# Third chunk's queries and keys ahead of the first gate product, row statistics of four chunks on ScalarE, small weight copies on VectorE

## The chip, the cores and the metric

The kernel runs on one core of one Trainium2 chip. The metric is the device time of one execution in microseconds. The kernel before takes 1048.6 us, the median of three runs (1048.55 to 1049.17). Engines are named as the profile names them: PE is TensorE's matmul (PEld its weight load), DVE is VectorE, ACT is ScalarE, POOL is GpSimd, SP is SyncE, which here issues the DMAs.

## The reference

2048 rows of 576 values go through two kinds of layer in turn, A, B, A, B, each on a layer norm of its input and with the input added back. A is attention with 32 heads of 18 values; a row looks at itself and at seven rows before it, two apart. B is two wide projections multiplied with each other and projected back.

```python
def _A_ref(x, wqkv, wo):                      # x: 1 x 2048 x 576, wqkv: 576 x 1728
    q, k, v = ...                             # 32 heads of 18
    idx = pos[:, None] - arange(8) * 2        # the rows that a row looks at
    logits = einsum("bhsd,bhswd->bhsw", q, kg) * 18 ** -0.5
    attn = softmax(where(idx >= 0, logits, -1e9))
    return einsum("bhsw,bhswd->bhsd", attn, vg).reshape(B, S, D) @ wo

def _B_ref(x, w_gate, w_up, w_down):          # F = 4608
    return ((x @ w_gate) * (x @ w_up)) @ w_down

x = x + _A_ref(_layernorm(x), A_wqkv, A_wo)
x = x + _B_ref(_layernorm(x), B_w_gate, B_w_up, B_w_down)
x = x + _A_ref(_layernorm(x), A_wqkv, A_wo)
x = x + _B_ref(_layernorm(x), B_w_gate, B_w_up, B_w_down)
```

## The kernel before

**Tiling.** The rows are cut into tiles of 128. An attention job j takes one tile (j = 0 and 1) or two (j = 2 and up); this text calls job j the chunk j + 1, so j = 2 is the third chunk. `seq` lists the jobs: rows 0, 1, 2 to 3, then 4 to 5, 6 to 7 of the first layer pair, then chunks of the second pair and the first in turn. The gated layer B follows: `first_pair` for the first two chunks, `small` for chunks 3 to 5, `big` for 512 rows at a time after that.

**A chunk of attention** (`attention`, L525 to L963) has these steps:

- `head` (L419): layer norm and transposition. Per tile DVE takes two `bn_stats` over 288 columns and a `bn_aggr` (L424, L426). ACT makes rstd of all the tiles of the chunk as exp(-0.5 ln(var + eps)) (L430, L431). The tile is normalised by DVE (L448) if `dve` is set, otherwise by ACT (L442, L443), and transposed by PE through a PSUM bank with a copy by ACT (L460, L463) if `on_pe` is set, otherwise by a DMA that SP issues (L453). `head` runs twice per chunk: in front of the attention (LN1) and in front of layer B (LN2).
- `project` (L580): q, k and v by products with the permuted weight `wqkv`, each with four full parts of the contraction and a tail of 64 rows. For j = 0 and 1 they are written out in place (L599). For later chunks they are units (`as_unit`, L543, products at L551) that are put among the gate products of layer B, at places that `IN_GU` names.
- logits: DVE multiplies q with shifted k (L744, four products with two shifts each); PE sums over the head's values with the selection matrix `Esel` (L760); softmax on DVE and ACT (L798, L785, L828 or L841, L837, L846 to L852); PE spreads the weights to the head's values with `Bsel` (L863); DVE multiplies with v and adds (L912, L928). For j = 0 PE adds them up (L916, L917), and the division by the softmax sum comes at the end (L931, L934) with 1/sum from L834 to L836, spread at L879 and copied at L883.
- output projection with `wo_p` (L479 for j = 0, L951 otherwise), the input added, and the second `head`; for j = 0 all this is `tail_fast` (L468 to L512).

**Layer B.** A unit (`g_unit`, L1038) makes a gate and an up product in two PSUM banks (L1046, tails L1056), ACT copies the gate (L1000), ACT and DVE or DVE alone multiply (L1002 to L1005). `batch` (L1014) puts the 64-row tails of neighbouring units together. In `first_pair` the first `SOLO` = 6 units are made for the first chunk alone with 128 columns each product, then six joint units for both chunks with 256 columns, then six for the second chunk alone; the down products follow (L1100, L1101).

**The start.** `wqkv` arrives as five blocks of rows, k = 0 to 4, and its columns are permuted by copies (`permute`, L338; the copies run at L351): per k one for queries (t3 = 0), one for keys (1), a small one of 128 columns for the last two values of every head's queries and keys (3), and later the values (2, 4). POOL also makes the identity, zeros, `Esel` and `Bsel` (`mk_sel`, L368) and the mask `cap` (`mk_cap`, L381).

**What sets the order.** Every operation is given to a planner (`Plan`) with engine, a cost in ns, keys that it reads and writes, a priority (smaller goes first) and sometimes an operation that it must follow (`after`). `Plan.run` walks through time and always issues the operation that can start first, by its costs; ties go to the smaller priority, then to the older operation. Each engine then runs its operations in that fixed order, waiting where data are late. Operations of PE in layer B form a chain (`bb`, L981, `chain["pe"]`), so their order is that of the program. `warm` (L965, matmuls at L967) fills planned waits of PE with products on the identity until the first product of the chain. PSUM banks come from pools: "unit" (two pairs), "boot" (three banks), "pa" (one bank at first) and "ring" (all of them later); `hand_over` moves banks into the ring. The costs and the order of priorities around the change:

```python
cost = {"DVE": 50 + 35 * nd, "ACT": 60 + 64 * nd, "POOL": 200 + 106 * nd}[eng]
op("POOL", 3200, mk_sel, w=["sel"], prio=1)
LN1P = {2: 1.5, 3: 3, 4: 2, 5: 2.5, 6: 2.5, 7: 3, 8: 1, 1: 0.4}
ATP = {1: 3, 2: 2.5, 3: 2.5, 4: 3, 5: 3, 6: 2}
```

Of the kernel before, what the change touches and what calls it, by code (L numbers as in the profile page):

```python
# [10 lines left out]
ALU = mybir.AluOpType  # L11
# [130 lines left out]
def kernel(  # L142
# [34 lines left out]
    KACT, VENG = (1, 4), ('POOL', 'POOL', 'ACT', 'ACT', 'ACT')  # L177
# [5 lines left out]
    BLK, JOB_AT, SOLO = 4, (0, 2), 6  # L183
# [147 lines left out]
    def setup_b():  # L331
# [6 lines left out]
        def permute(k, t3, eng, prio, d0=0, nd=16, **kw):  # L338
            if t3 < 3:
                src = (wrav[:, k, :] if t3 == 2 else wraw[:, k, t3 * D:(t3 + 1) * D]).rearrange("p (h d) -> p d h", h=H)[:, d0:d0 + nd, :]  # L340
                dst = wqkv[:, k, t3 * 512 + d0 * H:t3 * 512 + (d0 + nd) * H].rearrange("p (d h) -> p d h", h=H)
                cost = {"DVE": 50 + 35 * nd, "ACT": 60 + 64 * nd, "POOL": 200 + 106 * nd}[eng]
            else:
# [3 lines left out]
                cost = {"DVE": 80 + 75 * m, "ACT": 160 + 130 * m, "POOL": 250 + 180 * m}[eng]  # L347
# [38 lines left out]
        op("POOL", 3200, mk_sel, w=["sel"], prio=1)  # L386
# [11 lines left out]
        op("POOL", 0, swap, r=[f"wq{t}_{k}" for t in (0, 1, 3) for k in range(KT)],  # L398
# [20 lines left out]
    def head(src, keys, nst, dst, dkeys, prio, ab, on_pe, mg, first=None, then=None, dve=False):  # L419
# [9 lines left out]
        def rs():  # L429
            nc.scalar.activation(rstd[:, 0:nst], mv[:, 0:nst, 1], ACT.Ln, bias=eps_t[:])  # L430
            nc.scalar.activation(rstd[:, 0:nst], rstd[:, 0:nst], ACT.Exp, scale=-0.5)  # L431
        op("ACT", 490, rs, r=mk + ["eps"], w=[f"rstd{ab}"], prio=prio, after=then)
        if not dve:
            o = op("DVE", 210, lambda: nc.vector.scalar_tensor_tensor(nmr[:, 0:nst], mv[:, 0:nst, 0], -1.0, rstd[:, 0:nst],
# [4 lines left out]
        for i in range(nst):  # L439
# [4 lines left out]
            if dve:  # L444
                def apply_v(i=i):
                    x = src(i)
                    for c, d_, m in ((0, 0, D), (KF * P, D, TL)):
                        nc.vector.tensor_scalar(xn[i][:, d_:d_ + m], x[:, c:c + m], mv[:, i, 0:1], rstd[:, i:i + 1], op0=ALU.subtract, op1=ALU.mult)  # L448
                op("DVE", 420, apply_v, r=[keys[i], *mk, f"rstd{ab}"], w=[f"xn{ab}{i}"], prio=prio)
# [75 lines left out]
    def attention(j, la, t0, nst, units=None):  # L525
# [5 lines left out]
        on_pe, pe_sum = j < 4, j < 2  # L531
        prio, mg = (1, 0) if fast else (ATP.get(j, 3), 200 if j < 5 else 1500)
# [5 lines left out]
        head(lambda i: xin[:, i0 + i, :], xin_k, nst, xnT_A, xk, LN1P.get(j, prio), 0, j < 3, mg, None,marks["evq"] if j == 1 else None, j < 3)  # L538
# [41 lines left out]
        def project(tag, au, bu, tl, ea, eb, dkeys):  # L580


            if units is not None:
# [32 lines left out]
            if fast:  # L616
# [14 lines left out]
                def values():  # L631
# [9 lines left out]
                    for cost, fn, w_, eng in eb[2:]:  # L641
                        op("ACT", cost, lambda fn=fn: fn(ub, 0), r=[kb, "uv"], w=w_, prio=0.5, free="unit", use=ub)
# [95 lines left out]
        for p_ in range(W // 2):  # L738
# [27 lines left out]
            op("DVE", 60 + 5.6 * n, l1, r=qk, w=[pk], prio=lprio, after=marks["xb1"] if j == 1 and p_ == 3 else None)  # L766
# [35 lines left out]
        else:  # L802
# [20 lines left out]
            op("DVE", 100 + 7 * n, gather_l, r=[f"part{jj}" for jj in range(4)] + ["cap"], w=["Lt"], prio=prio - 1, margin=2500 if j < 5 else 3000)  # L823
            op("DVE", 240 + 4.5 * n, soft1d, w=["Lt", "mx", "rg"], prio=prio - 1)
        if fast:
            late["values"]()
            rz = xn_[1][1]
            op("ACT", 170 + 1.8 * n, lambda: nc.scalar.activation(late["a_c"][:, 0:W * sq], late["Lt"][:, 0:W * sq], ACT.Exp),  # L828
               r=["Lt"], w=["ac"], prio=0)

# [25 lines left out]
        if on_pe:  # L856
# [15 lines left out]
            if fast:  # L872
# [499 lines left out]
```

## Time and profile before

| | |
|---|---|
| median of three runs | 1048.6 us (1048.55 to 1049.17) |
| the profiled execution's own time | 1048.55 us |
| its span, first to last instruction | 1046.7 us |
| mean granted clock of PE | 0.998 |
| first gate product (L1046) starts | 33.54 us |
| PE busy from 34 to 100 us | 65.76 of 66 us |
| products on the identity (L967) | 107, 10.4 us |
| DMA | 135.5 MB, mean 129 GB/s |

A line of the profile's groups names the line of the code, the engine, the operation, what is written and what is read with shapes, the count, then the busy time and the mean of one, and the idle time of the engine in front of it with the one who ended it. In an order of time, a row has start and length in us; a square bracket behind it is the engine's idle time before it and its releaser. Matmul rows overlap, since they are pipelined: sixteen products of 128 columns start one behind the other in 0.89 us, though each row shows some 0.22 us.

### The profile page before, as it was taken

The page shows a single profiled execution, that of the slowest core. Times are in us where ns is not written, and L with a number is a line of the kernel's source. Part 1 is how long each engine was busy: PE and PEld are TensorE (multiplying, and loading weights), DVE is VectorE, ACT ScalarE, POOL GpSimd, SP SyncE. Part 2 cuts the span into 40 slices and gives each one's busy share as a digit, 9 for nine tenths or more (in the row PEclk, how much of TensorE's full clock was granted, in tenths as well). Part 3 has the DMA queues.
Part 4 walks back from the last instruction along what each step waited for, and adds up shares of the span by engine and source line. Part 5 has one row for each costly group of instructions (what it writes and reads, how often), then busy time and mean ns, then how long its engine had stood idle before and what let it go on. Part 6 is the DMA issues. An engine that isn't in the chain of part 4 may idle for free.

```text
span 1046.7 us, 19602 instructions
## 1 busy us (share of the span) xinstructions
PE 1028.5 (98%) x7898; PEld 595.9 (57%) x8016; DVE 723.0 (69%) x1366; ACT 446.3 (43%) x905; POOL 14.5 (1%) x54
## 2 busy tenths in 40 slices
PE   7999999999999999999999999999999999999998
PEld 6886886777765445554455544564455644554444
DVE  7896797889849886396766967579684796832211
ACT  4663763554645641354424443154531444214420
POOL 5000000000000000000000000000000000000000
PEclk9999999999999999999999999999999999999999
DMA  8918117454743805455143641635435352454212
GB/s 241 327 69 194 51 41 229 109 130 149 176 123 101 227 12 147 126 158 177 48 127 94 189 133 51 160 67 181 134 85 159 100 165 85 122 152 136 68 49 88
DMA packets 139834, 135.50 MB, mean 129 GB/s; under 512 B 43360, under 2 KB 137440, under 8 KB 139744
## 3 DMA queue, kind: packets, MB, share of 16 engines
q1 hardware_dynamic: 139744, 134.25, 45.0%
q8 instruction: 62, 1.02, 0.4%
q14 instruction: 28, 0.23, 0.1%
HBM read 114.49 MB, written 10.88 MB: 120 GB/s over the span
## 4 chain that ended last, share of the span: by engine, by line
PE 96%; issue 1%; DVE 1%; POOL 1%; ACT 0%; POOLq 0%; DVEq 0%
PE pu L1046 20%; PE pg L1046 18%; PE pg L1100 9%; PE pu L1100 8%; PE acct L1046 6%; PE pg L551 5%; PE pa L1046 4%; PE pu L551 4%; PE acct L1100 3%; PE pu L1056 3%; PE pg L1056 3%; PE pa L1100 2%; PE pg L1101 2%; PE pu L1101 2%; PE pa L951 1%
## 5 line engine op out<-in xcount | busy, mean ns | idle before, releaser
L1046 PEld LDWEIGHTS <-reg 128*128 128x128 bf16 x3072 | 277.5, 98 | 222.6 <-issue 24.2
L1046 PE MATMUL pu<-xnT_B,reg 128*128 128x512 bf16 (+2 forms) x1302 | 231.4, 316 | 1.3 <-issue 0.3
L1046 PE MATMUL pg<-xnT_B,reg 128*128 128x512 bf16 (+2 forms) x1204 | 220.4, 319 | 1.0 <-issue 0.2
L1100 PEld LDWEIGHTS <-reg 128*128 128x128 bf16 x864 | 84.4, 98 | 101.5
L1000 ACT CAST g_sb<-pu 128x512 bf16<-128x512 f32 x112 | 65.5, 588 | 126.3 <-PE pg L1056 66.2
L1003 DVE TENSOR_TENSOR reg<-reg,g_sb 128x512 bf16<-128x512 bf16 x144 | 59.7, 419 | 86.2 <-ACT reg L1002 76.6
L551 PEld LDWEIGHTS <-wqkv 128*128 128x128 bf16 (+1 forms) x1050 | 88.2, 97 | 34.0 <-issue 18.2
L744 DVE TENSOR_TENSOR prod<-qT,kT 128x2560 bf16<-128x2560 bf16 (+1 forms) x68 | 95.8, 1411 | 8.2 <-ACT kT L671 7.3
L912 DVE TENSOR_TENSOR prod<-vT,ab 128x1280 bf16<-128x1280 bf16 (+1 forms) x120 | 92.1, 776 | 0.0
L1000 ACT CAST g_sb<-pg 128x512 bf16<-128x512 f32 x112 | 65.8, 589 | 60.6 <-PE pu L1056 29.9
L928 DVE TENSOR_TENSOR qT<-qT,prod 128x1280 bf16<-128x1280 bf16 (+1 forms) x112 | 89.7, 801 | 2.5
L1101 PEld LDWEIGHTS <-reg 128*128 128x128 bf16 x864 | 84.9, 98 | 1.0
L430 ACT ACTIVATE rstd<-mv,eps_t 128x2 f32<-128x2 f32 (+1 forms) x33 | 9.8, 297 | 162.8 <-DVE mv L426 159.9
L1046 PE MATMUL acct<-xnT_B,reg 128*128 128x512 bf16 (+1 forms) x303 | 69.4, 354 | 0.5 <-issue 0.3
L551 PE MATMUL pg<-xnT_A,wqkv 128*128 128x256 bf16 (+1 forms) x500 | 69.6, 273 | 0.0
L1056 PE MATMUL pu<-xnT_B,reg 64*128 64x512 bf16 (+2 forms) x331 | 67.7, 316 | 0.1
L1101 PE MATMUL pu<-wd,reg 128*128 128x64 bf16 x336 | 64.8, 193 | 0.8
L1100 PE MATMUL pg<-wd,reg 128*128 128x512 bf16 x231 | 64.5, 380 | 0.0
L1056 PE MATMUL pg<-xnT_B,reg 64*128 64x512 bf16 (+2 forms) x305 | 62.8, 319 | 0.0
L551 PE MATMUL pu<-xnT_A,wqkv 128*128 128x256 bf16 (+1 forms) x410 | 59.1, 273 | 0.1
L1046 PE MATMUL pa<-xnT_B,reg 128*128 128x512 bf16 (+1 forms) x211 | 54.2, 376 | 0.6 <-issue 0.2
L1100 PE MATMUL pu<-wd,reg 128*128 128x512 bf16 x200 | 54.7, 380 | 0.0
(232 smaller groups left out, 1439.4 us busy)
## 6 DMA issues: line engine op xcount, KB each, us to landing
wd<-in_B_w_down_dram SPq DMA_DIRECT2D x152, 288.0 KB, 3.4
reg<-in_B_w_gate_dram SPq DMA_DIRECT2D x24, 768.0 KB, 4.8
reg<-in_B_w_up_dram SPq DMA_DIRECT2D x24, 768.0 KB, 6.3
reg<-in_B_w_down_dram SPq DMA_DIRECT2D x28, 288.0 KB, 3.3
s_dram<-s SPq DMA_DIRECT2D x13, 512.0 KB, 3.2
rg<-s_dram SPq DMA_DIRECT2D x52, 128.0 KB, 3.2
ab<-a_dram SPq DMA_DIRECT2D x52, 128.0 KB, 2.7
reg<-in_B_w_gate_dram SPq DMA_DIRECT2D x24, 96.0 KB, 5.6
```

The costliest lines, as they stand in the source:

```text
L430: nc.scalar.activation(rstd[:, 0:nst], mv[:, 0:nst, 1], ACT.Ln, bias=eps_t[:])
L551: nc.tensor.matmul(ring[use[p_]["slot"]][0:m, e * n:(e + 1) * n], lhsT=wqkv[r_, k, c0:c0 + m], rhs=xnT_A[r_, k, 0:n], start=start, stop=st ...
L744: nc.vector.tensor_tensor(late["prod"][lp(p_)][:, :, :, 0:n], q2, k2, op=ALU.mult)
L912: nc.vector.tensor_tensor(js(dst), js(vT[:, :, o0:o0 + n]), abw, op=ALU.mult)
L928: op("DVE", 60 + 3 * n, lambda tmp=tmp: nc.vector.tensor_tensor(oT[:, :, 0:n], oT[:, :, 0:n], tmp(), op=ALU.add), r=[pvk], w=ok, prio=prio)
L951: nc.tensor.matmul(b()[:, 0:HD], lhsT=oT[:, t, i * P:(i + 1) * P], rhs=wo_p[:, t, hh * HD:(hh + 1) * HD], start=(t == 0), stop=(t == KT - 1))
L1000: op("ACT", 590, lambda: nc.scalar.copy(g_sb[gs][:, 0:ul], bk(0)[:, 0:ul]), r=[keys[0]], w=[f"g{gs}"], prio=0, **fg)
L1003: op("DVE", 340, lambda: nc.vector.tensor_tensor(dst, dst, g_sb[gs][:, 0:ul], op=ALU.mult), r=[f"g{gs}"], w=[dk], prio=0)
L1046: nc.tensor.matmul(ring[use[q]["slot"]][:, e * n:(e + 1) * n], lhsT=w_[:, k], rhs=xT[:, k], start=(first and k == 0 and e == 0), stop=(las ...
L1056: nc.tensor.matmul(ring[use[q]["slot"]][:, e * n:(e + 1) * n], lhsT=w_[r_], rhs=xT[r_, KF], start=(fresh and e == 0), stop=not fresh, skip ...
L1100: nc.tensor.matmul(bank_of(i)[:], lhsT=lhs, rhs=wt[:, ft % 2, 0:512], start=first and not plus, stop=last_)
L1101: nc.tensor.matmul(tail_of(i), lhsT=lhs, rhs=wt[:, ft % 2, 512:D], start=(first and i == 0), stop=last_, skip_group_check=True)
```

## The change

The queries and keys of the third chunk (`PRE = 'q'`) are no longer units among the gate products: they are written out in the PE chain ahead of the first gate product. Their `head` may begin after the operation `weights` (1/sum of the first chunk). LN1 of chunks 2 to 5 (`LN1_S`) takes its row statistics on ACT, in two passes per tile with the accumulated output: the negated mean, then the sum of squares around it. The small copies of the weight go from POOL to DVE, the keys of k = 3 from DVE to ACT, and of the keys of k = 4 one half from ACT to POOL. LN2 of chunks 3 and 4 is transposed by DMA instead of PE (`LN2_PE` = 2 where 4 stood). `SOLO` is 7. The sixth and seventh chunk's units go to other places (`IN_GU`). The spread of 1/sum is written behind the fourth value product of the first chunk. Costs and priorities change.

```diff
-    KACT, VENG = (1, 4), ('POOL', 'POOL', 'ACT', 'ACT', 'ACT')
+    KENG = {1: ("ACT", "ACT"), 3: ("ACT", "ACT"), 4: ("ACT", "POOL")}
+    VENG = ('POOL', 'POOL', 'ACT', 'ACT', 'ACT')
+    LN1_PE, LN2_PE, ATT_PE, LN2_V, L1_LATE, MG, MGD = 3, 2, 4, 3, 3, 200, 3000
+    LN1_V = (0, 1, 2)
+    LN1_S, LN2_S = (1, 2, 3, 4), ()
+    PRE, SUM_PE = 'q', 2
+    LN1_AFTER = {1: "evq", 2: "weights"}
...
-    BLK, JOB_AT, SOLO = 4, (0, 2), 6
+    BLK, JOB_AT, SOLO = 4, (0, 2), 7
...
-                if t3 == 1 and k in KACT:
-                    for d0 in (0, 8):
-                        permute(k, t3, "ACT", 1.5, d0, 8)
+                if t3 == 1 and k in KENG:
+                    for d0, e_ in zip((0, 8), KENG[k]):
+                        permute(k, t3, e_, 1.5, d0, 8)
...
-                    permute(k, t3, "POOL" if t3 == 3 and k < KF else "DVE", 1.5)
+                    permute(k, t3, "DVE", 1.5)
...
-        op("POOL", 3200, mk_sel, w=["sel"], prio=1)
+        op("POOL", 3200, mk_sel, w=["sel"], prio=0.5)
...
+        def sums(i):
+            nc.scalar.activation(xn[i][:, 0:D], src(i), ACT.Copy, scale=-1.0 / D, accum_out=mv[:, i, 0:1])
+
+        def squares(i):
+            nc.scalar.activation(xn[i][:, 0:D], src(i), ACT.Square, bias=mv[:, i, 0:1], accum_out=mv[:, i, 1:2])
         for i in range(nst):
+            if act:
+                op("ACT", 820, lambda i=i: sums(i), r=[keys[i]], w=[f"sm{ab}{i}", f"mv{ab}{i}", f"xn{ab}{i}"], prio=prio, after=first)
+                op("ACT", 860, lambda i=i: squares(i), r=[keys[i], f"sm{ab}{i}"], w=[f"mv{ab}{i}", f"xn{ab}{i}"], prio=prio)
+                continue
...
-                op("DVE", 420, apply_v, r=[keys[i], *mk, f"rstd{ab}"], w=[f"xn{ab}{i}"], prio=prio)
+                op("DVE", 620, apply_v, r=[keys[i], *mk, f"rstd{ab}"], w=[f"xn{ab}{i}"], prio=prio)
...
-    LN1P = {2: 1.5, 3: 3, 4: 2, 5: 2.5, 6: 2.5, 7: 3, 8: 1, 1: 0.4}
-    ATP = {1: 3, 2: 2.5, 3: 2.5, 4: 3, 5: 3, 6: 2}
-    LPP = {1: 2.5, 2: 2, 3: 2.5, 4: 1.5, 5: 1.5, 6: 2}
+    LN1P = {1: 1.6, 2: 2, 3: 2.5, 4: 2.5, 5: 3, 6: 2.5, 7: 3, 8: 1.5}
+    ATP = {1: 2.5, 2: 2.5, 3: 3, 4: 2, 5: 2.5, 6: 1.5}
+    LPP = {1: 2.5, 2: 2.5, 3: 2.5, 4: 1.5, 5: 1.5, 6: 1.5}
...
-            if units is not None:
+            if units is not None and tag not in pre:
...
-        head(lambda i: xs_f[:, i0 + i, :], fk, nst, xT, xTk, (1 if j > 1 else 0.5) if j < JSM + 2 else prio - 1, 1, j < 4, mg, None, None, j < 3)
+        head(lambda i: xs_f[:, i0 + i, :], fk, nst, xT, xTk, (1 if j > 1 else 0.5) if j < JSM + 2 else prio - 1, 1, j < LN2_PE, mg, None, None, j < LN2_V, j in LN2_S)
...
+    if PRE:
+        early[2] = []
+        gens[2] = prepare(2, early[2], PRE)
+        next(gens[2])
...
-    IN_GU, IN_D = {0: {3: [2]}, 2: {0: [3], 7: [4]}, 3: {2: [5], 12: [6]}}, {}
+    IN_GU, IN_D = {0: {3: [2]}, 2: {0: [3], 7: [4]}, 3: {0: [5], 13: [6]}}, {}
```

More of the change, by code (lines that the diff above doesn't have):

```diff
@@ L397, in swap @@
             late["ab"] = rot.tile([P, 4, 2 * CH], BF16, name="ab")
-        op("POOL", 0, swap, r=[f"wq{t}_{k}" for t in (0, 1, 3) for k in range(KT)],
+        op("DVE", 0, swap, prio=0, r=[f"wq{t}_{k}" for t in (0, 1, 3) for k in range(KT)],
            w=["prod0", "prod1", "s10", "s11", "s12", "s13", "Lt", "ab", "ac", "rg"])
@@ L926, in attention, with spread_z, rzs @@
                     marks["sum"] = op("PE", 330, gather, r=[pvk, "ident"], w=[bo[0].key, bo[1].key], prio=0)
+                if i_ == 3:
+                    late["total"]()
+                    br = Bank()
+                    def spread_z():
+                        for e in range(4):
+                            for h_ in range(2):
+                                nc.tensor.matmul(br()[:, e * sq:(e + 1) * sq], lhsT=Bsel[:, e].rearrange("p a b -> p (a b)"),
+                                                 rhs=rz[:, h_ * sq:(h_ + 1) * sq], start=(e == 0 and h_ == 0), stop=(h_ == 1), skip_group_check=True)
+                    op("PE", 350, spread_z, r=["zs", "xn11", "sel"], prio=0, **br.take())
+                    def rzs():
+                        return late["Lt"][:, 2 * P:2 * P + n]
+                    op("ACT", 300, lambda: nc.scalar.copy(rzs(), br()[:, 0:n]), r=[br.key, "Lt"], w=["rzs"], prio=0.5, **br.drop())
             elif i_:
```

62 lines of the change are left out of this document (31 added, 31 removed).

## The prediction

> **What bounds the kernel now.** I read the page's busy shares first, then its chain of work that ended last, then the busy time by stage, then the order of time of the first 60 us.
>
> ```profile
> PE 1028.5 (98%) x7898; PEld 595.9 (57%) x8016; DVE 723.0 (69%) x1366; ACT 446.3 (43%) x905; POOL 14.5 (1%) x54
> PE 96%; issue 1%; DVE 1%; POOL 1%; ACT 0%; POOLq 0%; DVEq 0%
> ```
>
> TensorE (PE) carries 96% of the chain. The stages say where the rest is. Columns: window, length, then busy time of PE, PEld, DVE, ACT, POOL (in the last two rows PE alone), granted clock, DMA share, GB/s.
>
> ```profile
> 7.00:10.50 3.50, 0.61 (x8) 0.43 (x7) 3.15 (x7) 1.21 (x2) 3.44 (x15) 1.00 0.89 257
> 12.00:14.00 2.00, 2.00 (x23) 1.61 (x22) 0.12 (x1) 0.15 (x1) 2.00 (x9) 0.50 0.63 186
> ...
> 34.00:100.00 66.00, 65.76 (x877) 1.00 0.62 178
> 100.00:200.00 100.00, 99.58 (x939) 1.00 0.40 104
> ```
>
> From 34 us on PE misses 0.2 us in 66 and 0.4 in 100, and its list of waits there adds up to 1.2 us. So the time is the moment at which the first gate product starts, plus all PE work behind it. Only two things can help: an earlier or fuller start, and less PE work behind it. The start in order of time:
>
> ```profile
> 8.95 0.70 POOL L374 TENSOR_SCALAR_AFFINE_SELECT Bsel<-Bsel 128x128 bf16<-128x128 bf16 x1
> ...
> 10.51 1.10 POOL L351 COPY wqkv<-wraw 128x128 bf16<-128x128 bf16 x3
> 10.58 0.23 PE L599 MATMUL pu<-xnT_A,wqkv 128*128 128x128 bf16 x1 [2.97 <-POOL xf L307]
> ...
> 13.85 0.60 ACT L705 ACTIVATE qT<-pg 128x512 bf16<-128x512 f32 x1 [4.01 <-PE pu L599]
> ```
>
> The square bracket is the idle time before the row and who ended it. PE stands 2.97 us because GpSimd (POOL), which copies the small weight columns, first finishes the selection matrices: they run from 3.40 to 10.2 us, where the code's plan counts 3.2 us. The second stretch is ahead of the first gate product:
>
> ```profile
> 27.94 1.18 DVE L448 TENSOR_SCALAR xn<-xf,mv,rstd 128x576 bf16<-128x576 bf16 x4
> 29.03 0.82 DVE L744 TENSOR_TENSOR prod<-qT,kT 128x1280 bf16<-128x1280 bf16 x1
> 29.77 0.46 DVE L481 BATCH_NORM_STATS2 st<-pu 128x6 f32<-128x288 f32 x1
> 30.45 0.83 PE L967 MATMUL pa<-ident 128*128 128x128 bf16 x12 [0.78 <-ACT xnT_A L463]
> 33.54 1.09 PE L1046 MATMUL pg<-xnT_B,reg 128*128 128x128 bf16 x16
> ```
>
> L967 is padding on the identity. Between 27.9 and 33.5 PE does 1.3 us of output projection (first chunk), two transpose groups of 0.28, three groups of logit sums of about 0.25, one product of 0.28 on the identity, and else pads or waits: some 2.7 us are free.
>
> **The change part by part, on the profiled execution (1048.55 us; span 1046.7; the runs' median is 1048.6, so the same).**
>
> *Small copies to DVE, keys of k=3 to ACT, half of k=4 to POOL.* DVE loses one 128x512 copy (0.53 of a row of 8 in 4.26) and gains four small ones of 0.27 (the fifth is there already): +0.5, so its copies end at about 9.9 instead of 9.46, with the last weights in at 8.63. ACT does k=3 instead of one half of k=4: +0.6, in its idle stretch before 8.63. POOL loses four copies (0.40 each) and gains one of 128x256: between 0.40 (128x128) and 1.09 (128x512), on that line 0.63. It is queued behind the selection matrices (10.2), a memset of 0.09 and the cap memsets (0.55), so it ends near 11.4. PE can do k=0 to 3 before, and needs this piece for the nine closing products only: 11.65 to 12.3 instead of 13.20 to 13.85. **-1.5**. From one side -0.5 (POOL slower under the added DVE copies), from the other -3.5 (selections at their short rows' 0.7 and 0.25 us end at 8.4; then DVE's 9.9 decides). I take the middle one, because nothing in the change touches the selections. The granted clock is 0.50 from 11.5 to 15.0, behind the idle stretch, and that is why the nine products take 0.65 us. [...]
>
> *Row statistics on ACT for chunks 2 to 5.* Per 128-row tile DVE loses two rows of 0.44 and one of 0.21, 1.1 us; ACT gains two passes over 128x576. Nearest rows: the copy L463 of 128x640 at 0.69 and the normalisation L442 of 128x576 at 0.86; so 0.65 to 1.06 each, if reading the sum out is one more instruction at the 0.20 of the shortest row (L431). I take 0.86, the row of the same shape. [...] On the first chunk's path it frees DVE by a little: statistics stand directly ahead of the softmax maximum (18.73 to 19.54, maximum at 19.57). ACT's three value-weight copies now come before the second chunk's rstd (its priority goes from 0.4 to 1.6), so the transposed copy of the second chunk (0.69) lands at about 18.4, ahead of the exponential: +0.5 there, and -0.6 since the second chunk's normalisation (0.63 on DVE) no longer splits the four logit products. Together 0. Third chunk: four passes, 3.4 us, between 20.7 and 25.5 in ACT's idle 1.41, 1.44 and 0.92 us; its rstd is ready by about 26, as before (26.99).
>
> *The tail of the first chunk.* L448 now carries 620 instead of 420 in the plan (the rows say 0.43 + 0.29 less overlap, 0.6). With that the second chunk's product L744 at 29.03 falls behind the statistics it now holds up by 0.75 us. **-0.5**, between 0 and -0.8. First chunk ready for its gate product at 33.5 - 1.5 - 0.5 = 31.5.
>
> *Third chunk's q and k ahead of it.* In the profile they stand in L551: eight groups of four at 0.44, and four closing pairs at 0.11: 3.94 us of PE. They need both transposed tiles. Normalised at 26.4 to 27.6 (L448 less 1.5), tile one transposes behind the output projections (27.7), its copy takes 0.69, tile two uses the same PSUM bank (29.0), and its copy falls behind the first chunk's normalisation on ACT (30.4 to 31.1). So PE starts q and k at 31.1 and, with a group of logit sums between, the first gate product follows at 35.4, by order of the PE chain. The start moves from 33.5 to 35.4, **+1.9**; the work behind it loses **-3.94**, and one group of logit sums and one of transposes that now stand in 33.5 to 36.4 (0.24 + 0.28, **-0.5**).
>
> *Second normalisation of chunks 3 and 4 by DMA transposes.* 20 transposes on PE (L460) at 0.055 go: **-1.1**; four copies of 0.69 on ACT too. SP gains four transposes (1.2 to issue, 3.1 to land). Chunk 3 is normalised at 96.4 and used by PE at 110.4: covered by 10 us. Chunk 4 is normalised at 172.6, used at 176.0, so up to 1 us would show; but the sixth chunk's projections move in front (position 2 to 0), 7.2 us as the fourth chunk's take from 102.99 to 110.19. Weight loads queued behind on SP have eight buffers in flight. 0; without the cover +1 to +2.
>
> *Seven solo units instead of six.* 64 products of 128 columns (0.89 for 16) for 32 of 256 (0.87 for 8): **+0.1**. It also moves the first joint unit 2.0 us of PE work later, behind 3.94 less.
>
> *Priorities, margins, order of spread and swap.* No instruction more; 0, covered by PE's fullness.
>
> Sum: -1.5 - 0.5 are inside the +1.9; so +1.9 - 3.94 - 0.5 - 1.1 + 0.1 = -3.5, of which I give 0.2 to new PE bubbles: -3.3, **1045.3 us**.
>
> **Rivals.**
>
> *Fuller start.* POOL's selections are quick or the tile copies come earlier: -3.5 instead of -1.5 and q and k 1 us earlier: 1042.3. For: the selection of 2.50 us stands among rows of 0.7. Against: DVE is as full beside it as before. 0.18.
>
> *It does not do what it says.* Tile two of the third chunk loses its bank. In the profile it did: tile one at 29.23, then the second chunk's logit sums hold the bank until 36.05 and tile two comes at 35.95, in another. Then q and k start at 35.6 and the gate product at 39.5: +6.0 - 3.94 - 0.5 - 1.1 + 0.1 = +0.5, 1049.1. The middle between this and the forecast, about 1047.5, is a start that is only not hidden. Against: two normalisations in a row before the second chunk's product. 0.21.
>
> *Slower.* Second chunk late at the first joint unit:
>
> ```profile
> 55.05 0.69 ACT L463 COPY xnT_B<-pa 128x640 bf16<-128x640 bf16 x1 [0.59 <-PE pa L460]
> ...
> 56.07 0.27 PE L1056 MATMUL pg<-xnT_B,reg 64*128 64x256 bf16 x1
> ```
>
> Only 0.3 us lie between the copy's end (55.74) and its use. DVE is busy 18.9 of 20 us in 40 to 60. With q and k some 9 us earlier, the third chunk's logit work (1.49 + 0.69 + 0.8, four times, 12 us) is ready amid the second chunk's value products (40.75 to 48.07), at equal priority. PE reaches the joint unit 22.5 (33.5 to 56.0) - 3.9 + 2.0 = 20.6 us behind 35.4, at 56.0; the second chunk is ready at 55.7 less 2, so 2.3 us of reordering are free. If three rounds more go first, 9 us less 2.3 show: -3.3 + 6.7, 1052. Against: equal priority goes to the older work, the second chunk. 0.14.
>
> **Numbers.** Forecast, 1043.5 to 1046.5: 0.44; fuller start 0.18; not as said 0.21; slower 0.14; the rest, 0.03, slower. A measurement of this kernel tells about 0.2%, 2.1 us, from no change: faster 0.62, same 0.21, slower 0.17. The range, 1041.5 to 1050.0, leaves out the slower case and the end of the fuller start.
>
> **What would show it.** Nine closing products near 11.7 (not 13.2); no padding between 28 and 35; q and k of L599 ahead of the first L1046, that one near 35.4; first joint L1056 at 56 with no wait; no L460 behind 60 us; waits of PE behind 36 us still near 1 us. Wrong if the first L1046 comes past 38, or if a wait stands ahead of the joint unit or of the fourth chunk's first product.

## The result and the profile after

The changed kernel takes 1050.26 us (median; 1049.44 to 1052.1), the kernel before beside it 1048.57 us (1047.82 to 1051.0). The ratio is 1.0019, 95% interval 1.0011 to 1.0026: slower by 0.19%, at the bound of what can be told from no change. 1045.3 was forecast, and the range ended at 1050.0. The profiled execution of the changed kernel took 1049.64 us with a span of 1047.9 us, 1.2 us more than before. Seven runs lie at 1049.4 to 1050.4 us and five at 1051.6 to 1052.1 at a mean clock lower by 0.001 to 0.003, of which no trace was kept; the profile is one of the seven, so the 1.2 us are what the traces have to explain.

Line numbers move by some 20: q, k and v in place are L616 (were L599), units of q, k and v L568 (L551), gate products and tails L1068 and L1078 (L1046, L1056), down products L1122 (L1100), padding L989 (L967), transposes and their copies L476 and L479 (L460, L463), the sums of logits L778 (L760). The chain of work that ended last in the changed kernel:

```profile
PE 95%; DVE 2%; issue 1%; POOL 1%; DMA 1%; ACT 1%; SPq 0%; DVEq 0%; POOLq 0%
```

DVE now holds 2% of the chain (1% before). By stage (window, length, busy time of PE, PEld, DVE, ACT, POOL, clock, DMA share, GB/s):

```profile
0.00:34.00 34.00, 25.94 (x472) 22.18 (x472) 24.71 (x58) 23.85 (x57) 12.84 (x51) 1.00 0.91 275
34.00:100.00 66.00, 65.79 (x929) 52.70 (x923) 49.58 (x98) 41.33 (x90) 0.00 (x0) 1.00 0.65 182
100.00:200.00 100.00, 99.58 (x937) 74.60 (x944) 83.48 (x142) 51.25 (x106) 0.00 (x0) 1.00 0.43 111
200.00:250.00 50.00, 47.27 (x430) 34.75 (x435) 38.16 (x75) 24.87 (x51) 0.00 (x0) 1.00 0.52 141
```

The first 34 us no longer hold a stretch at half clock. From 34 to 200 us PE is as full as before. Between 200 and 250 us it misses 2.7 us. That is new; in the kernel before it misses 0.4:

```profile
200.00:250.00 50.00, 49.60 (x455) 36.49 (x460) 41.96 (x75) 22.64 (x46) 0.00 (x0) 1.00 0.59 166
```

The start of the changed kernel, in order of time (in square brackets the idle time and who ended it):

```profile
4.21 4.16 PE L989 MATMUL pa<-ident 128*128 128x128 bf16 x44 [4.21 <-POOL ident L322]
...
8.21 0.44 PE L476 MATMUL pu<-ident,xn 128*128 128x128 bf16 x5
...
12.16 0.23 PE L616 MATMUL pg<-xnT_A,wqkv 64*128 64x128 bf16 x1
...
31.19 0.83 PE L989 MATMUL pa<-ident 128*128 128x128 bf16 x12 [0.91 <-ACT xnT_A L479]
31.86 0.44 PE L519 MATMUL pg<-ident,xn 128*128 128x128 bf16 x5
32.49 0.61 PE L616 MATMUL pg<-xnT_A,wqkv 128*128 128x256 bf16 x4
...
37.75 1.06 PE L1068 MATMUL pg<-xnT_B,reg 128*128 128x128 bf16 x16
```

The identity comes at 4.2 us instead of 1.3, since the selection matrices now stand ahead of it in POOL's queue. The 44 paddings that wait for it hold the first transposes until 8.21; in the kernel before they come here:

```profile
5.44 0.44 PE L460 MATMUL pu<-ident,xn 128*128 128x128 bf16 x5
```

The nine closing products start at 12.16 (13.20 before), the third chunk's q and k at 32.49, and the first gate product at 37.75 instead of 33.54: 4.2 us later. That start is not the same in every profile: seven that share its code up to that product (this one and those of the experiments that touch nothing in front of it) have it at 37.71 to 38.49.

The other loss is new. DVE and PE around 242 us in the changed kernel:

```profile
226.89 1.56 DVE L920 TENSOR_TENSOR prod<-vT,ab 128x1280 bf16<-128x1280 bf16 x2 [4.83 <-DMA ab<-a_dram]
...
244.01 0.42 DVE L1025 TENSOR_TENSOR hb<-hb,g_sb 128x512 bf16<-128x512 bf16 x1
...
244.49 0.39 PE L1122 MATMUL pa<-wd,hb 128*128 128x512 bf16 x1 [2.41 <-DVE hb L1025]
```

PE stands 2.4 us because DVE, busy without a gap from 226.89 us, makes the product of gate and up of a unit, which the down products read, only at 244.0. In the kernel before, DVE's work in the same place starts earlier, with the seventh chunk's logit products:

```profile
225.02 1.49 DVE L744 TENSOR_TENSOR prod<-qT,kT 128x2560 bf16<-128x2560 bf16 x1 [2.65 <-ACT kT L671]
```

The balance of the two spans, with the forecast's terms for the work behind the start and two measured numbers (start and new wait): +4.2 (start) - 3.94 (q and k no longer behind) - 0.5 (logit sums and transposes of that stretch) - 1.1 (transposes by DMA) + 0.1 (solo units) + 2.4 (new wait) = +1.2 us, as measured (1047.9 - 1046.7). That it closes tests the four forecast terms only as a sum; the transposes alone are measured further below.

### The profile page after: what moved, and what is told of

Read it like the earlier page. It is cut to its first block, busy times and chain, and to the rows that moved or that the text cites. A ratio compares the mean times of both kernels' runs of the same rounds, so it can differ in the third digit from the quotient of the medians.

```text
span 1047.9 us, 19683 instructions
## 1 busy us (share of the span) xinstructions
PE 1025.8 (98%) x7929; PEld 593.8 (57%) x8047; DVE 717.8 (69%) x1348; ACT 454.0 (43%) x930; POOL 12.8 (1%) x51
## 4 chain that ended last, share of the span: by engine, by line
PE 95%; DVE 2%; issue 1%; POOL 1%; DMA 1%; ACT 1%; SPq 0%; DVEq 0%; POOLq 0%
PE pu L1068 19%; PE pg L1068 18%; PE pg L1122 9%; PE pu L1122 8%; PE pa L1068 6%; PE acct L1068 4%; PE pg L568 4%; PE pu L568 4%; PE pa L1122 3%; PE pu L1078 3%; PE pg L1078 2%; PE acct L1122 2%; PE pg L1123 2%; PE pu L1123 2%; PE acct L973 1%; PE pa L1078 1%
## 5 line engine op out<-in xcount | busy, mean ns | idle before, releaser
L1068 PEld LDWEIGHTS <-reg 128*128 128x128 bf16 x3104 | 278.5, 98 | 221.3 <-issue 23.9
L1068 PE MATMUL pu<-xnT_B,reg 128*128 128x512 bf16 (+2 forms) x1318 | 231.2, 314 | 1.3 <-issue 0.3
L1068 PE MATMUL pg<-xnT_B,reg 128*128 128x512 bf16 (+2 forms) x1220 | 220.3, 317 | 1.0 <-issue 0.2
L1122 PEld LDWEIGHTS <-reg 128*128 128x128 bf16 x864 | 84.5, 98 | 101.6
L568 PEld LDWEIGHTS <-wqkv 128*128 128x128 bf16 (+1 forms) x1010 | 84.7, 97 | 33.4 <-issue 17.8
L1068 PE MATMUL pa<-xnT_B,reg 128*128 128x512 bf16 (+1 forms) x303 | 69.4, 354 | 0.5 <-issue 0.3
L1078 PE MATMUL pu<-xnT_B,reg 64*128 64x512 bf16 (+2 forms) x335 | 67.6, 314 | 0.1
L568 PE MATMUL pg<-xnT_A,wqkv 128*128 128x256 bf16 (+1 forms) x475 | 66.1, 273 | 0.0
L1122 PE MATMUL pg<-wd,reg 128*128 128x512 bf16 x231 | 64.4, 380 | 0.0
L1078 PE MATMUL pg<-xnT_B,reg 64*128 64x512 bf16 (+2 forms) x309 | 62.9, 316 | 0.0
L568 PE MATMUL pu<-xnT_A,wqkv 128*128 128x256 bf16 (+1 forms) x395 | 57.0, 273 | 0.1
L1068 PE MATMUL acct<-xnT_B,reg 128*128 128x512 bf16 (+1 forms) x211 | 54.2, 375 | 0.6 <-issue 0.2
L1122 PE MATMUL pu<-wd,reg 128*128 128x512 bf16 x200 | 54.7, 380 | 0.0
```

Of the source, the lines that this page charges most:

```text
L568: nc.tensor.matmul(ring[use[p_]["slot"]][0:m, e * n:(e + 1) * n], lhsT=wqkv[r_, k, c0:c0 + m], rhs=xnT_A[r_, k, 0:n], start=start, stop=st ...
L1068: nc.tensor.matmul(ring[use[q]["slot"]][:, e * n:(e + 1) * n], lhsT=w_[:, k], rhs=xT[:, k], start=(first and k == 0 and e == 0), stop=(las ...
L1078: nc.tensor.matmul(ring[use[q]["slot"]][:, e * n:(e + 1) * n], lhsT=w_[r_], rhs=xT[r_, KF], start=(fresh and e == 0), stop=not fresh, skip ...
L1122: nc.tensor.matmul(bank_of(i)[:], lhsT=lhs, rhs=wt[:, ft % 2, 0:512], start=first and not plus, stop=last_)
```

## The experiments

The kernel before ran beside every one of them, at medians of 1048.5 to 1049.1 us; ratios are to it. "Changed" is the kernel after the change.

### Identity first

Diff, on the changed kernel:

```
-        op("POOL", 3200, mk_sel, w=["sel"], prio=0.5)
+        op("POOL", 3200, mk_sel, w=["sel"], prio=1)
```

> The changed kernel with the selection matrices back at priority 1, so that GpSimd makes the identity and the zeros first. Theory: in the changed kernel PE's 44 paddings wait for the identity (4.21 us) and hold the first transposes until 8.21; with the identity first the paddings begin near 1.4, the transposes near 5.5, the nine closing products near 11.2 instead of 12.16, and the first gate product near 36.8 instead of 37.75: about 1049.3 (1 us under the changed kernel). Rival, my forecast's reckoning: the selections then run among the weight copies, GpSimd's half of k = 4 comes near 11.4, the closing products at 11.7: only 0.5 us, about 1049.8. If the selections are as slow as before the change and nothing else: 1050.3 or more.

Measured: 1052.87 us (1050.34 to 1054.34), ratio 1.0037 (1.0024 to 1.0050). The closing products did come at 10.44 us instead of 12.16, but then PE stood idle for 2.21 us and soon for 0.88 more, and ran at half clock behind that. PE's row at 14 us and the stage behind it:

```profile
14.16 0.40 PE L616 MATMUL pg<-xnT_A,wqkv 128*128 128x128 bf16 x4 [2.21 <-POOL wqkv L357]
```

```profile
15.50:26.00 10.50, 9.42 (x130) 7.95 (x131) 6.24 (x14) 3.97 (x10) 0.24 (x1) 0.51 0.98 321
```

The clock column reads 0.51 for 10.5 us (1.00 before 15.5), and the first gate product came at 42.0 instead of 37.75. So an earlier start by itself can cost more than it brings. The wait for DVE that stood at 242 us stayed, 2.3 us.

### The planner's margin on all value products

The margin of an operation is a time that the planner waits, in its own reckoning, before it lets the operation start; others then go first.

```
-                   margin=0 if on_pe or i_ else 800 if j < 5 else 3500)
+                   margin=0 if on_pe else 800 if j < 5 else 3500)
```

> The changed kernel with the planner's margin of 3500 ns (800 for early chunks) on all eight value products of a chunk instead of the first one only, so that the sixth chunk's value products are not put ahead of the seventh chunk's logit products on DVE. Theory: DVE's wait of 4.83 us for the spread weights at 222 us goes, and with it PE's wait of 2.4 us at 242: 1047.9, span of the work behind the first gate product 2.4 us shorter. Rival: DVE is simply too full there, and another wait of 1 to 2.4 us takes its place: 1049.3 to 1050.3.

Measured: 1097.48 us, ratio 1.0462. The 242-us wait shrank to 0.3 us, but the same margin made later chunks late: PE's list of waits now has four kinds in front of gate and up products, 5.9 to 19.2 us in total each. This edit was too broad to answer the question; a narrower one follows below.

### No early q and k

```
-    PRE, SUM_PE = 'q', 2
+    PRE, SUM_PE = '', 2
```

> The changed kernel without the early projection: the third chunk's queries and keys are units among the gate products again (PRE is empty); all else as changed. Theory: the early projection fills almost no idle time, because PE gets both transposed tiles only at 31.2 and then also carries four groups of logit sums that were free before; the first gate product comes at 33.0 to 33.5 instead of 37.75 and the work behind it is 3.94 + 0.75 us longer, so the time is within 0.5 us of the changed kernel, 1049.8 to 1050.8. My forecast said that it hides 2.0 us: then 1052.3. Third: it costs (it delays the second chunk's attention): 1048.5 to 1049.5.

Measured: 1055.94 us (1053.53 to 1056.38), ratio 1.0064. Both the theory and the forecast's logic put too little on it. The first gate product came at 34.07, but the first joint unit waited for the second chunk:

```profile
59.01 0.27 PE L1078 MATMUL pg<-xnT_B,reg 64*128 64x256 bf16 x1 [1.94 <-ACT xnT_B L479]
```

The clock was 0.51 from 60 to 63.5 us. So the kernel without the early q and k is 5.7 us slower (1055.94 - 1050.26), but the trace does not lay that on the missing q and k alone. PE reached the joint unit at 57.1 us, the changed kernel at 57.3. The second chunk was later: ACT's copy of it started at 58.29 instead of 55.96, behind the statistics of a later tile, for whose rows ACT had first stood 1.62 us. The edit makes the planner write the order anew, and in the new order those two passes go ahead of the copy.

### The DMA transposes alone, in the kernel before

The second normalisation of chunks 3 and 4 transposed by DMA, all else as before:

```
-  ..., 1, j < 4, mg, None, None, j < 3)
+  ..., 1, j < 2, mg, None, None, j < 3)
```

> The kernel before with one part of the change alone: the second normalisation of chunks 3 and 4 transposed by DMA. Forecast's term: 20 transposes of 0.055 us leave PE, 1.1 us, 1047.5, with no new wait at 110 or 176 us. Rival: the fourth chunk's tiles land after the first gate product of that chunk is due (176.0; here its projections are not moved in front), and PE waits 0.5 to 1.5 us there: 1048.0 to 1049.0.

Measured: 1054.16 us, ratio 1.0050 (1.0037 to 1.0062). PE's two new waits:

```profile
102.59 0.38 PE L1100 MATMUL pu<-wd,hb 128*128 128x512 bf16 x1 [1.95 <-DMA wd<-in_B_w_down_dram]
180.77 1.03 PE L1046 MATMUL pg<-xnT_B,reg 128*128 128x256 bf16 x8 [2.23 <-DMA xnT_B<-xn]
```

Alone, the edit costs 5.5 us. The rival named the second wait: the fourth chunk's transposes land after its first gate product is due. The expectation had not named the first: SP issued four transposes at 95.3 to 101.1 us, two of them new, with a single load of down weights between them, and PE stood for weights. Behind that wait the clock was 0.50 for some 3.4 us, 1.7 us more. In the changed kernel neither wait exists. For the fourth chunk the sixth chunk's projections fill the time (173.9 to 181.1 us); what covers the weights there no run took apart.

### The margin on the sixth chunk alone

```
-                   margin=0 if on_pe or i_ else 800 if j < 5 else 3500)
+                   margin=0 if on_pe or (i_ and j != 5) else 800 if j < 5 else 3500)
```

> Changed kernel, with the planner's margin (800 to 3500 ns, until now on the first value product of a chunk) on all eight value products of the sixth chunk alone; only orders between 224 and 400 us of the plan move. Theory: the 2.4 us that PE waits at 242 us come from DVE standing 4.8 us in front of those products until the spread weights land by DMA; with the seventh chunk's logit products ahead of them, as in the kernel before, the wait goes: 1047.9 (1047.3 to 1048.5), no wait of PE over 0.5 us between 200 and 300 us. Rival: the wait only moves to another product (the whole order behind 224 us is PE-bound by DVE's work, not by its order): 1050.0 to 1050.5, with a wait of 1.5 us or more elsewhere in 224 to 420 us.

Measured: 1050.51 us, ratio 1.0015 (1.0006 to 1.0023). The rival held in that the wait moved: the 242-us wait fell to 0.4 us and a new one stood at 307 us, where a transposed tile was 3 us later:

```profile
306.95 1.02 PE L1068 MATMUL pg<-xnT_B,reg 128*128 128x512 bf16 x4 [1.66 <-issue]
```

### No padding behind 25 us, and with the margin

```
-                    self.warm(min(44, int(max(0, t - clock["PE"] - 100) / 100)))
+                    self.warm(min(44 if t < 25000 else 0, int(max(0, t - clock["PE"] - 100) / 100)))
```

> Changed kernel, no padding products behind 25 us; all else in the same order. Theory: the 23 paddings between 29.2 and 31.9 us wait for ACT's copies, since they write the same PSUM bank as the transposes, and hold up the third chunk's second tile and the first chunk's transposes by 0.5 to 0.65 us: first gate product at 37.2 instead of 37.75, time 1049.7 (1049.4 to 1050.0) if the later waits stay. Rival: the granted clock falls behind the longer idle time of PE (about 2.5 us in two pieces), first gate product then at 39 to 40: 1052.

Measured: 1052.17 us (1049.38 to 1054.96), ratio 1.0030. The third chunk's q and k started 0.4 us earlier (32.09), and then the clock fell; the first gate product came at 38.73:

```profile
26.00:36.00 10.00, 8.06 (x139) 5.39 (x137) 7.51 (x18) 5.52 (x17) 0.00 (x0) 0.84 1.07 336
```

> Changed kernel with both edits: the margin on the sixth chunk's eight value products, no padding behind 25 us. Theory: the two add up, -2.4 and -0.5: 1047.3 (1046.8 to 1048.0), below the kernel before by about 0.1%. Rival: one of the two moves a wait instead of taking it away: 1049.5 or more.

Measured: 1050.82 us, ratio 1.0018. In this profile the clock stayed at 1.00 and the first gate product came at 37.61, 0.1 us earlier than in the changed kernel. But both profiles without padding had come later to the third chunk's first transposes (28.30 and 28.57 instead of 28.01), for reasons ahead of the edit. From there to q and k PE took 4.48 us with the padding and 3.79 and 3.78 without it. So the padding holds the start up by 0.7 us, a little more than the theory said, and without it the clock fell in one profile and not in the other. The waits behind were as with the margin alone, 0.4 us at 242 and 1.6 at 307.

### Row statistics on DVE again

```
-    LN1_S, LN2_S = (1, 2, 3, 4), ()
+    LN1_S, LN2_S = (), ()
```

> Changed kernel with the row statistics of chunks 2 to 5 by bn_stats on DVE again, as before. The forecast put this part at 0, since DVE's work there is hidden. By it: 1050.3, first gate product within 0.5 us of 37.75. Rival: between 36 and 60 us DVE is the engine that decides when the second chunk is ready; DVE has 14 tiles of 1.1 us more ahead of that, of which the six of chunks 2 and 3 come before: a wait of 1 to 3 us ahead of the first joint unit (near 58 us) or a later third chunk, 1052 to 1054.

Measured: 1057.21 us (1055.32 to 1059.09), ratio 1.0082. Above even the rival's 1052 to 1054. PE's rows around the third chunk's tiles:

```profile
39.05 0.66 PE L989 MATMUL pa<-ident 128*128 128x128 bf16 x9 [0.78 <-ACT xnT_A L479]
44.13 1.06 PE L1068 MATMUL pg<-xnT_B,reg 128*128 128x128 bf16 x16
```

The third chunk's second tile is copied by 39.05 us instead of 31.2, and the first gate product comes 6.4 us later. The two tiles were normalised by 31.8 us (27.9 in the changed kernel), but PE wrote them into the bank `pa` only from 36.11, for the second chunk's logit sums had it first. The first product into that bank behind the sums waits until DVE has read them:

```profile
35.56 0.72 PE L989 MATMUL pa<-ident 128*128 128x128 bf16 x10 [1.00 <-DVE Lt L805]
```

That is the prediction's second rival, a tile of the third chunk that loses its bank. ScalarE's statistics bring the tiles ahead of those sums; a cost of 0 was right only for the kernel in which they do.

### DVE's order by hand

Two of DVE's instructions, the sixth chunk's second and third value product, are issued behind the seventh chunk's logit work; the plan itself is unchanged:

```
-            o.fn()
+            if o.idx in (984, 986):
+                held.append(o)
+            else:
+                o.fn()
+            if o.idx == 1184:
+                for h in held:
+                    h.fn()
```

> Changed kernel; every engine keeps the order and the plan of the changed kernel, except that DVE gets two instructions later: the sixth chunk's second and third value product now stand behind the seventh chunk's last logit work, where the kernel before has them. Theory: this takes the 2.4 us wait at 242 us away and nothing else changes, unlike the planner's margin, after which a new wait of 1.7 us stood at 305 us: 1048.0 (1047.5 to 1048.6), waits of PE behind 45 us below 1.5 us in all. Rival: DVE has too little time there whatever its order, and the wait stays at 1.5 us or more at 242 us or behind it: 1049.5 to 1050.3.

Measured: 1051.3 us (1049.23 to 1052.83); ratio 1.0016 (1.0007 to 1.0025). The theory falls. DVE now begins with the logit products, but they wait for the seventh chunk's keys until 226.73, and 1.9 of the 2.4 us stay:

```profile
244.32 0.39 PE L1128 MATMUL pa<-wd,hb 128*128 128x512 bf16 x1 [1.94 <-DVE hb L1031]
```

### Identity first, with the padding that covers the gap

Identity first as above, and

```
+ {109: 33, 110: 10}.get(o.idx, 0)   # more paddings ahead of two PE operations
```

> Changed kernel with identity and zeros ahead of the selection matrices, as in the earlier run with that edit, and with 33 more padding products behind the nine closing products and 10 more a microsecond later, so that PE does not idle there. Theory: the half clock from 15.5 to 26 us in that run came from the 3.3 us that PE stood idle ahead of it; with the padding the clock stays at 1.00 and the earlier start shows: first gate product at 37.0 to 37.5 instead of 42.0, time 1049.3 to 1049.8. Rival: the clock falls for another reason (the load of the closing products, or chance): 0.50 again for several us and 1052 to 1053.

Measured: 1052.35 us (1050.4 to 1054.13), ratio 1.0035. At the start the theory held: the clock was 1.00 throughout the first 60 us, the first gate product came at 37.33. The time did not follow, because of the other wait, 2.48 us here, and the clock behind it:

```profile
246.00:248.00 2.00, 2.00 (x11) 1.12 (x10) 2.00 (x5) 0.00 (x0) 0.00 (x0) 0.50 0.68 181
```

With 0.92 in the two microseconds before these and 0.72 in the two behind them, 2 x (0.08 + 0.50 + 0.28) = 1.7 us are lost beyond the 2.5.

> Changed kernel with both repairs: DVE's order by hand and identity first with the longer padding. Theory: the two add up: 1047.3 (1046.8 to 1048.0), 0.1% below the kernel before. Rival: the start's repair brings nothing since the first chunk is held by DVE's logit products beside POOL's value copies: 1048.0, as with the order alone.

Measured: 1051.58 us (1049.65 to 1053.28), ratio 1.0026. Neither the theory nor the rival came out. Its first part failed as it had alone: a wait of 1.9 us at 244 us, and the clock 0.97 between 200 and 250 us. And the start, with the code of the run before, came at 38.59 instead of 37.33.

### The place of the seventh chunk's projections

The change moves `IN_GU[3]` from `{2: [5], 12: [6]}` to `{0: [5], 13: [6]}`: the sixth chunk's units earlier, and the seventh chunk's one unit later. Put back, that one number, in the changed kernel:

```
-    ... 3: {0: [5], 13: [6]}}, {}
+    ... 3: {0: [5], 12: [6]}}, {}
```

> Changed kernel with one number back: the seventh chunk's projections among the gate products of unit 12, as in the kernel before, not of unit 13. Theory: DVE then starts that chunk's logit products 1.7 to 6 us earlier and PE no longer waits for it at 242 us: waits of PE behind 45 us 0.5 us or less in all, 1047.3 to 1048.0 in undisturbed clock, median 1047.9. Rival: DVE's order or its load is the cause, the wait stays at 1.5 us or more: 1049.5 to 1050.5.

Measured: 1047.65 us (1047.04 to 1050.59), ratio 0.9992 (0.9983 to 1.0001). DVE's start on that chunk and PE's stage:

```profile
222.48 1.49 DVE L762 TENSOR_TENSOR prod<-qT,kT 128x2560 bf16<-128x2560 bf16 x1 [4.98 <-ACT kT L689]
```

```profile
200.00:250.00 50.00, 49.77 (x456) 36.73 (x455) 41.98 (x81) 26.10 (x53) 0.00 (x0) 1.00 0.58 157
```

DVE starts this row of work 4.4 us earlier than in the changed kernel, and PE's waits behind 36 us are 0.2 and 0.2 us. One number made the difference, 2.3 us between the two spans and 2.6 between the medians, and the theory's range was met. This version beats the changed kernel (the two intervals do not touch); against the kernel before, a gain of 0.1% is likely and not settled.

> Kernel before with the one number of the change: the seventh chunk's projections at unit 13 instead of 12. Theory: a wait of PE for DVE of 1 to 2.5 us appears between 236 and 260 us, 1049.6 to 1051. Rival: nothing, since the kernel before runs about 1.3 us later against DVE there and its order hides it: 1048.5 to 1049.2.

Measured (before, with 12 turned to 13): 1050.89 us, ratio 1.0015 (1.0006 to 1.0023). The size of the theory, 1.8 us, but not its place: DVE's logit products start at 229.0 instead of 225.0, the down products behind them wait 0.4 us, and the longest wait is for a transposed tile at 308 us, near where the margin had moved it:

```profile
PE pg L1046 <- DMA xnT_B<-xn: 1.3, 1, 1.3
```

So the place of these units costs the time in either kernel; where it comes out depends on the order around it. The theory had the size from the trace and the place wrong.

> Changed kernel with the seventh chunk's projections at unit 12, identity and zeros ahead of the selection matrices, and the longer padding behind the closing products. Theory: first gate product at 37.2, no wait behind it: 1047.0 to 1047.8, 0.1% below the kernel before. Rival: the start varies from run to run (DVE and POOL side by side, clock), and the median is 1048.5 or above.

Measured: 1048.35 us (1047.18 to 1050.03), ratio 0.9994 (0.9985 to 1.0003). The median lies between the theory's range and the rival's bound, and the rival's reason is in the profile: the first gate product came at 38.74, 1.4 us later than in the first run with that start (37.33). One selection of 128x32 on POOL took 3.37 us beside DVE's weight copies (3.36 in the run with both repairs, 0.68 in the one at 37.33), and the closing products waited 1.61 us for the copy that POOL makes behind it. The start's repair brings nothing that can be relied on.

### Two terms of the sum, in the repaired kernel

On the kernel with the seventh chunk at 12, the second normalisation on PE again:

```
-    LN1_PE, LN2_PE, ATT_PE, ... = 3, 2, 4, ...
+    LN1_PE, LN2_PE, ATT_PE, ... = 3, 4, 4, ...
```

> Kernel of the run with the seventh chunk's projections at unit 12, and the second normalisation of chunks 3 and 4 transposed by PE again, as before the change. Forecast's term: the 20 transposes come back on PE, +1.1 us: 1048.8. Rival: DVE and ACT order behind 50 us moves with them and a new wait appears, 1050 or more.

Measured: 1048.88 us (1048.47 to 1049.38), ratio 1.0000 (0.9991 to 1.0009). Behind the first gate product stand 1047.3 - 38.28 = 1009.0 us against 1045.6 - 37.71 = 1007.9: 1.1 us, the forecast's term.

```
-    BLK, JOB_AT, SOLO = 4, (0, 2), 7
+    BLK, JOB_AT, SOLO = 4, (0, 2), 6
```

> Kernel of the run with the seventh chunk's projections at unit 12, and six solo units instead of seven. Forecast's term: 0.1 us less PE work, 1047.5, if the second chunk is ready for the first joint unit 2 us earlier (near 56 instead of 58 us). Rival: it is not, and PE waits 0.5 to 2 us ahead of the first joint unit, with the half clock behind it: 1048.5 to 1051.

Measured: 1054.4 us (1053.95 to 1055.99), ratio 1.0054. The rival held, and more than its price: the second chunk's copy starts at 57.30, the joint unit waits for it.

```profile
55.72 0.68 ACT L429 ACTIVATE xn<-xf 128x576 bf16<-128x576 bf16 x1 [1.72 <-DMA xf<-in_A_x_dram]
57.30 0.67 ACT L479 COPY xnT_B<-acct 128x640 bf16<-128x640 bf16 x1
58.02 0.37 PE L1078 MATMUL pg<-xnT_B,reg 64*128 64x256 bf16 x1 [2.44 <-ACT xnT_B L479]
```

PE had transposed the chunk by 55.0 us. Again ACT's order puts the statistics of a later tile, whose rows arrive only at 55.7, ahead of the copy. So the seventh solo unit gives the second chunk time, but the greater part of the wait is that order and not the chunk's own work.

## Why the prediction was wrong, point by point

- **What bounds the kernel** was right. In the repaired kernel the span is the start (37.71) plus 1007.9 us; before it was 33.54 plus 1013.2. The difference behind the start, -5.3 us, is the forecast's -3.94 - 0.5 - 1.1 + 0.1 = -5.4. The trace of the changed kernel missed the forecast by 4.5 us (+1.2 instead of -3.3): the two points that follow are 2.4 and 2.3 of it, less the 0.2 given to bubbles.
- **The step that failed: "Priorities, margins, order of spread and swap. No instruction more; 0, covered by PE's fullness."** An order is a set of due times. The forecast looked at the sixth chunk's units (position 2 to 0) and passed over the seventh's (12 to 13) in the same line. Their keys set when DVE's run of work can begin, some 17 us (226.9 to 244.0) that must end before PE's down products; PE's fullness was the thing at stake and covers nothing. The term measured 2.4 us in the profile, 2.6 us between the medians with 13 and with 12, and the same number cost 1.8 us in the kernel before. My first reading of the trace, DVE's order there, was not the cause: with the hand-made order 1.9 us stayed, and where the margin took the wait away it came out at 307 us.
- **The start was mis-sized: +1.9 forecast, +4.2 measured.** "Because nothing in the change touches the selections" was wrong: their priority went from 1 to 0.5, ahead of the identity. They ran fast there (128x128 in 0.31 us, against 0.69 to 2.50 in the kernel before), but the identity came late, the first transposes at 8.21 instead of 5.44, and the closing products won 1.0 us instead of 1.5. The third chunk's second tile was copied at 30.46 to 31.14, just as forecast (31.1), but q and k started at 32.49: padding (0.7 us), the first chunk's transposes (0.4) and a group of logit sums stood in front. They then took 5.3 us, with three groups of logit sums among them (0.26 each); the 0.5 that is left of 5.26 - 3.94 - 0.78 is, as an estimate, about 0.1 at each of the six changes between the two kinds of product. The forecast had counted 3.94 and one group, so 37.75 instead of 35.4. Three of the four groups had come before the first gate product in the kernel before too, in time that PE had free; now they stand on the path.
- **Row statistics: the size was right, the cover was not seen.** The passes measure 0.68 and 0.78 with 0.18 and 0.19 for reading the sum (0.86 forecast for each). At 0 us for the change as a whole this was fair; but taken out of this kernel by itself it is worth 6.9 us (1057.21 - 1050.26), since the third chunk then loses its bank.
- **DMA transposes, -1.1, right** (1.1 measured), with the cover that was named for the fourth chunk: alone in the kernel before, without it, that chunk's wait was 2.2 us ("+1 to +2"). The 5.5 us that the part cost there also hold 2.5 us of waits for down weights, which "eight buffers in flight" had put at nothing, and the half clock behind them.
- **Seven solo units, +0.1**, not measured alone as PE work, and blind to its use: with six the repaired kernel is 6.7 us slower, mostly through ACT's order.
- **The clock.** The prediction lays the 0.65 us of the nine closing products to the granted clock of 0.50. The changed kernel bears it out: at 1.00 they took 0.39 us (12.16 to 12.55). At what idle time the clock falls no run shows.
- **The rivals.** "Tile two loses its bank" did not happen; it came second in the same bank. It does happen with the statistics on DVE. "Second chunk late at the first joint unit" did not happen either, but it was near, with 0.7 us between the copy's end (56.66) and the first joint product (57.34): it is what came when the early q and k, or the seventh solo unit, were taken out. The slower case had the right shape, DVE late for PE, and the wrong place, 58 us instead of 242. None of the signs named for "wrong" (first gate product past 38, a wait ahead of the joint unit or of the fourth chunk) came true; of the signs named for "right", the closing products near 11.7, no padding between 28 and 35 and about 1 us of waits behind 36 us failed. The forecast looked for trouble up to the fourth chunk, in the first 180 us, and the new wait stands at 242.

## What to carry to other kernels

Read every number of an order that a change edits as a due time, and follow it to the engine that works between it and the product that needs it; a full engine shows that the old dates held, not that there is room. Parts of a change that cost nothing together can each be worth several microseconds when one is taken out or put in alone (here 5.5 to 6.9): one is the cover of another, and a planner that writes the order anew puts other work in front. So read in the trace what now stands ahead of the late operation before a price is laid on the part. Identity first moved the first gate product from 37.75 us to 42.0 with PE idle behind the closing products (clock 0.51), and to 37.33, 38.59 and 38.74 in the three runs with the longer padding there (clock 1.00 from 10 to 36 us): with PE kept busy the clock stayed, but the time was no lower for it (1052.35 us against 1050.26, 1051.58 against 1051.3, 1048.35 against 1047.65).

## What the runs showed of the hardware

**Half clock behind some waits of PE and not behind others.** Waits of 2.2 us and then 0.9 (identity first) were followed by 10.5 us at 0.51, of 1.9 us (no early q and k) by 3.5 us at 0.51, and of 2.48 us (identity first, padded), 2.44 (six solo units) and 1.95 (transposes alone) each by a loss of 1.7 us, some 3.4 us at 0.50. In the run without late padding the clock was 0.84 from 26 to 36 us, with no wait over 0.94 there, and 1.00 with the same waits and the margin. Waits of 1.94 us (order by hand), 2.41 (changed kernel), 2.7 (statistics on DVE) and 2.8 (no late padding) were followed by none, and the kernel before showed both: half clock in its own profile after 2.97 us, none after 2.71 at the same place in the run with the transposes alone. The length of the wait did not tell which.

**POOL's and DVE's instructions took longer side by side.** With DVE idle, POOL's selections of 128x128 took 0.31 us each (1.5 to 3.1 us in the changed kernel); in the kernel before, beside DVE's weight copies, 0.69 to 2.50. One of 128x32 took 0.21 alone and 3.37 beside the copies (seventh chunk at 12 with the early start). And DVE's four logit products, in the changed kernel and with the early start (identity first, padded), where POOL copies value weights (until 14.7 us) beside the first of them:

```profile
14.05 3.17 DVE L762 TENSOR_TENSOR prod<-qT,kT 128x1280 bf16<-128x1280 bf16 x4 [0.41 <-ACT qT L716]
```

```profile
11.99 4.87 DVE L762 TENSOR_TENSOR prod<-qT,kT 128x1280 bf16<-128x1280 bf16 x4 [0.41 <-ACT qT L716]
```

1.22 us each instead of 0.79. They start 2.1 us earlier and end 0.4 us earlier (16.86 instead of 17.22): most of what the earlier start won went there.

**The sum of a ScalarE pass is read by an instruction of its own**, 0.18 and 0.19 us here. The two passes over one tile in the changed kernel:

```profile
11.36 0.68 ACT L429 ACTIVATE xn<-xf 128x576 bf16<-128x576 bf16 x1
11.95 0.18 ACT L429 ACTIVATION_READ_ACCUMULATOR xn<-xf 128x1 f32 x1
12.16 0.78 ACT L432 ACTIVATE xn<-xf,mv 128x576 bf16<-128x576 bf16 x1
12.85 0.19 ACT L432 ACTIVATION_READ_ACCUMULATOR xn<-xf,mv 128x1 f32 x1
```
